# A second feed-forward layer whose first product goes by a 2x2x2 Strassen scheme over pairs of chunks and of token blocks, with its weights converted right behind the attention

## The chip, the cores and the metric

The kernel runs on one core of one Trainium2 chip. The metric is the device time of one execution in microseconds, as the median of several runs. The kernel's output is the transposed result of the last layer.

## What is computed

A linear attention with decay over 4 batches, 8 heads, 768 positions and 48 dimensions gives x (3072 tokens x 384). Two feed-forward layers follow, each with d_model 384 and d_ff 2048; they differ in the gate:

```python
state = zeros(B, H, D, D)
for t in range(S):
    cur = (u * k[t]) outer v[t]
    y[t] = r[t] @ (state + cur)
    state = w[t] * state + k[t] outer v[t]
x = y as (B*S, H*D)
h = x @ w_in1;  x = (h * clip(h + 3, 0, 6) / 6) @ w_out1
h = x @ w_in2;  out = (h * sigmoid(h)) @ w_out2
```

All inputs are float32. The feed-forward products use the fp32r form of TensorE. To keep the accuracy, every operand is held as two parts: a high part (the value rounded by a copy into fp32r) and a low part (the value less the high part). A product of two such operands is three matmuls: high by high, high by low, low by high.

## The kernel before

**Tiles.** The tokens are cut into six blocks j of 512 (four batches of 128 positions); the attention works through 24 groups of 128 tokens. Each layer cuts d_ff into 16 chunks fc of 128 and d_model into three k-chunks of 128. All feed-forward matmuls but those of the start are 128x128 by 128x512. For one block and one chunk, `mm1` (L842, matmuls at L858) makes the hidden tile h in a PSUM bank with 3 k-chunks x 3 = 9 matmuls; the gate and `split` (L886) make the high part gh and the low part gl; `mm2` (L865, matmuls at L880) adds them into three accumulators of 128 output columns with 9 more. PSUM has eight banks here: two of tag "h" for the hidden tiles, three "att" and three "acc" for attention and accumulators.

**Stages.** Attention groups (`attention`, L604) are interleaved with the first layer's blocks (`block1`, L900). The first layer's result goes to a DRAM scratch `x2d` and comes back with `load_x2` (L927), which makes its high and low parts. `block2` (L941) is the second layer: 6 blocks x 16 chunks x 18 matmuls, its gate one pass of ACT (L950) and then a cast (L891) and a subtraction (L893) on DVE.

**Weights.** A chunk of both weights of a layer arrives as pairs of 32-bit words; `load_w` (L466) turns them into float32 with three DVE passes over 768 columns (L32, L38, L44) and `split_w` (L499) into high and low parts with an ACT copy (L504) and a DVE subtraction (L505). The first `LATE_W = 4` chunks (L510) of the second layer go to a pool of their own, the rest into slots that the first layer's weights leave. All of them wait for `last_att` (L995): in the kernel before, all work planned up to the fifth block of the first layer.

**Checks.** `check_decay` (L792, two ACT passes at L800) and `check_weights` (L808) look for inputs out of the supported range while the second layer runs; a one-column matmul at the end makes a flag of them.

**Order.** Nothing is issued in the order of the source. Every piece of work is an `op` with a cost in ns for each engine that may do it and a key (its due place), and `Plan.order` (L263) fixes the order of each engine beforehand. It simulates the engines with these costs and, for an engine that comes free, takes among the operations that could start first the one with the smallest key:

```python
first = min(t for t, _ in able)
t, op = min((x for x in able if x[0] <= first), key=lambda x: (x[1].key, x[1].n))
```

A buffer slot is free when its last user has ended by that count. So a changed cost or key moves instructions on every engine. In `block2` the key of chunk fc of block j is 16 * (6 + j) + fc, and its second product stands `MM2 = 1.5` later, so that on PE the second product of one chunk follows the first product of the next.

Of the kernel before, what the change touches and what calls it, by code (L numbers as in the profile page):

```python
# [344 lines left out]
def tile_decay_attention_mlp2(  # L345
# [26 lines left out]
    C = 128  # L372
# [93 lines left out]
    def load_w(layer, fc, key, where="wp", after=(), whole=False):  # L466
# [28 lines left out]
        wts[layer, fc] = (val,)  # L495
        if not whole:
            split_w(layer, fc, key, where)

    def split_w(layer, fc, key, where="wp"):  # L499
# [290 lines left out]


    def check_decay(g, key, after):  # L792
        ws = Part(new("late", "cw", 2, [PD, SEQ + 1], f"cw{g}"))
        op({"SP": 470}, key - 2, lambda e: e.dma_start(out=ws.ap, in_=wseq_in[g]),
           writes=[ws], data=2000.0, after=after)
        off = Part(new("late", "off", 1, [PD, NP, C], f"off{g}"))

        def reach(e):
            for i, sign in enumerate((1.0, -1.0)):
                e.activation(  # L800
                    off.ap, ws.ap[:, 0:SEQ].rearrange("p (a b) -> p a b", b=SEG)[:, :, 1:],
                    AF.Relu, scale=sign, bias=-W_REACH - sign,
                    accum_out=stray.ap[:PD, 2 * g + i:2 * g + i + 1],
                )

        op({"ACT": 1560}, key, reach, [ws], [off, stray])
# [117 lines left out]
                out=x2d[j].ap[:, c, :], in_=x2.ap  # L924
            ), [x2], [x2d[j]], data=730.0)

    def load_x2(j, key, after):  # L927
        raw = Part(new("late", "xr", 2, [128, KC, N], f"xr{j}"))
        op({"SP": 470}, key, lambda e: e.dma_start(out=raw.ap, in_=x2d[j].ap),
           [x2d[j]], [raw], data=2200.0, after=after)  # L930
        new_x(1, j)
        xh, xl = x_parts[1, j]
        op({"DVE": 960, "ACT": 1450}, key + 1, lambda e: (
            e.activation(xh.ap, raw.ap, AF.Copy) if e is nc.scalar
            else e.tensor_copy(xh.ap, raw.ap)
        ), [raw], [xh])
        op({"DVE": 1755, "POOL": 4200}, key + 1, lambda e: e.tensor_tensor(
            xl.ap, raw.ap, xh.ap.bitcast(F32), op=ALU.subtract
        ), [raw, xh], [xl])

    def block2(j, key):  # L941
        acc = [
            Part(new("ps", "acc" if j % 2 else "att", 3, [128, N], f"acd{j}_{c}"))
            for c in range(KC)
        ]
        for fc in range(FC):
            kk = key + fc
            h = mm1(1, j, fc, kk)
            g = Part(new("gp", "g", 2, [128, N], f"g2_{j}_{fc}"))
            op({"ACT": 595}, kk, lambda e, g=g, h=h: e.activation(g.ap, h.ap, AF.Silu), [h], [g])  # L950
            gh, gl = split(g, f"2_{j}_{fc}", kk, {"DVE": 430}, {"DVE": 690})
            turn = {FC - 3: (-0.5, 0.05, 0.1), FC - 2: (0.2, 0.3, 1.4), FC - 1: (1.2, 1.3, 1.5)}
            mm2(1, fc, gh, gl, acc, kk + MM2, [
                key + FC - 1 + x for x in turn.get(fc, ())
            ] if j == NCH - 1 else ())
        for c in range(KC):
            o = Part(new("late", "o", 3, [128, N], f"o{j}_{c}"))
            op({"ACT": 595, "DVE": 690}, key + FC, lambda e, c=c, o=o: (
                e.activation(o.ap, acc[c].ap, AF.Copy) if e is nc.scalar
                else e.tensor_copy(o.ap, acc[c].ap)  # L960
            ), [acc[c]], [o])
            op({"SP": 470}, key + FC, lambda e, c=c, o=o: e.dma_start(
                out=out_t[c * 128:(c + 1) * 128, :].rearrange("p (b s) -> p b s", b=B)[
                    :, :, j * C:(j + 1) * C
                ],
                in_=o.ap.rearrange("p (b s) -> p b s", b=B),
            ), [o], data=730.0)


    MM2 = 1.5  # L970
    WHOLE = (0,)
    WHOLE_FC = 8
    loads = {g: load_group(g, FIRST + g) for g in range(B)}
    begun = [o for o in plan.ops if "SP" in o.engs]
    begun[0].data += 450.0
# [4 lines left out]
    for j in range(NCH):  # L980
        new_x(0, j)
        for i in range(B):
            key = -100.0 + i if j == 0 else FC * (j - 1) + (j == 1) * 3.0 + i * 3.3
            attention(j * B + i, key)
        if j == 0:
            for fc in range(FC):
                if fc == WHOLE_FC:
# [11 lines left out]
    for fc in range(LATE_W, FC):  # L999
        load_w(1, fc, FC * (NCH - 1) + 2 + 2 * fc)  # L1000
    for j in range(NCH):
        load_x2(j, FC * (NCH + j) - 6.0, last_att)
        block2(j, FC * (NCH + j))
    begin = FC * (NCH + 1)
    for i in range(NG):
        check_decay(i, begin + 2.5 * i, last_att)
    if WW == 2:
        for i in range(2 * FC):
            check_weights(i // FC, i % FC, begin + 1 + 2 * i, last_att)


    total = Part(flags.tile([128, 1], F32, name="total"))
    ones = Part(flags.tile([128, 1], F32, name="ones"))
    bad = Part(flags.tile([1, 1], I32, name="bad"))
    late = FC * (2 * NCH - 1) + 3.0
    op({"DVE": 100}, late, lambda e: e.memset(ones.ap, 1.0), [], [ones], after=last_att)
    op({"DVE": 230}, late, lambda e: e.tensor_reduce(total.ap, stray.ap, axis=AX.X, op=ALU.add),
       [stray], [total])
    op({"DVE": 150}, late, lambda e: e.tensor_scalar(total.ap, total.ap, 0.0, None, op0=ALU.is_le),
       [total], [total])  # L1020
    pf = Part(new("ps", "att", 3, [1, 1], "pf"))
    op({"PE": 60}, late, lambda e: e.matmul(pf.ap, total.ap, ones.ap, start=True, stop=True),
       [total, ones], [pf])
    op({"DVE": 150}, late, lambda e: e.tensor_scalar(bad.ap, pf.ap, 128.0, None, op0=ALU.is_lt),
       [pf], [bad])
# [101 lines left out]
```

## Time and profile before

| | before |
|---|---|
| median of 3 runs | 913.15 us (912.92 to 913.53) |
| the profiled execution | 913.38 us |
| its span (first to last instruction) | 911.7 us |
| PE busy | 902.6 us, 99% of the span |
| DVE busy | 570.7 us, 63% |
| ACT busy | 331.6 us, 36% |
| POOL busy | 62.1 us, 7% |
| TensorE clock granted | 0.998 |

The profile comes from one execution. Busy times are sums over an engine's instructions; matmuls are pipelined, so that the time of one matmul in a list of groups is longer than its step in a row of them. PEld is the weight load of TensorE, which overlaps the matmuls. A wait shows as idle time before an instruction, with the instruction that ended it.

### The profile page before, as it was taken

To read this page: it belongs to the slowest core of one execution; us is meant where nothing else is said; L and a number is where in the kernel's file an instruction comes from. 1 tells how busy PE (TensorE), PEld (TensorE's weight loads), DVE (VectorE), ACT (ScalarE), POOL (GpSimd) and SP (SyncE) were. 2 spreads that over 40 slices of the span, in tenths; PEclk is the share of its full clock that TensorE was granted. 3 is DMA by queue.
4 is the path that set the end of the run, shared out by engine and by line. 5 is a ranking of instruction groups with operands and counts; after the bars stand their busy time and mean duration, and the time that the engine had idled before them with its cause. 6 is when DMAs were issued, how large, how long until landed. Compare 5 with 4: busy or idle time off the path is not lost.

```text
span 911.7 us, 13804 instructions
## 1 busy us (share of the span) xinstructions
PE 902.6 (99%) x5570; PEld 721.7 (79%) x5570; DVE 570.7 (63%) x926; ACT 331.6 (36%) x785; POOL 62.1 (7%) x52
## 2 busy tenths in 40 slices
PE   9999999999999999999999999999999999999997
PEld 7546778888888878888888888888888888888886
DVE  8999999867676766664478878544544543222221
ACT  6645474314332332331145756323233321212111
POOL 1514003100020110000000000000000000000000
PEclk9999999999999999999999999999999999999999
DMA  9945324313221311110076765644644500100001
GB/s 304 362 119 167 127 75 128 108 44 94 89 87 43 109 42 41 65 33 1 24 242 190 217 202 173 202 150 162 208 140 169 176 35 1 35 1 6 30 1 36
DMA packets 39604, 101.11 MB, mean 111 GB/s; under 512 B 3697, under 2 KB 16113, under 8 KB 39537
## 3 DMA queue, kind: packets, MB, share of 16 engines
q1 hardware_dynamic: 39536, 100.20, 34.1%
q8 instruction: 44, 0.72, 0.3%
q14 instruction: 24, 0.19, 0.1%
HBM read 90.75 MB, written 9.44 MB: 110 GB/s over the span
## 4 chain that ended last, share of the span: by engine, by line
PE 91%; DVE 7%; issue 1%; ACT 0%; POOL 0%; DVEq 0%; POOLq 0%; ACTq 0%
PE h L858 41%; PE acd L880 22%; PE acc L880 19%; PE py L720 3%; PE pa L641 2%; PE filler L588 1%; DVE val L38 1%; PE pkv L753 1%; PE acc L871 1%; PE pk L654 1%; DVE val L44 1%; DVE g L913 1%; DVE spare L707 0%; DVE pre L616 0%; DVE val L32 0%
## 5 line engine op out<-in xcount | busy, mean ns | idle before, releaser
L858 PE MATMUL h<-x,w 128*128 128x512 f32 x1584 | 390.4, 391 | 0.0
L858 PEld LDWEIGHTS h<-x,w 128*128 128x128 f32 x1584 | 295.8, 188 | 62.4 <-issue 0.4
L891 DVE CAST gh<-g 128x512 fp32r<-128x512 f32 x161 | 70.5, 438 | 196.0 <-ACT g L950 191.7
L880 PE MATMUL acd<-gh,w 128*128 128x512 f32 x576 | 192.7, 389 | 0.0
L880 PE MATMUL acc<-gh,w 128*128 128x512 f32 x528 | 180.2, 393 | 0.0
L950 ACT ACTIVATE g<-h 128x512 f32<-128x512 f32 x96 | 57.5, 599 | 260.1 <-PE h L858 235.9
L893 DVE TENSOR_TENSOR gl<-g,gh 128x512 fp32r<-128x512 f32 x184 | 128.6, 701 | 4.8 <-ACT gh L890 0.3
L880 PEld LDWEIGHTS acd<-gh,w 128*128 128x128 f32 x576 | 108.1, 188 | 22.5
L911 ACT ACTIVATE g<-h 128x512 f32<-128x512 f32 x96 | 57.2, 596 | 180.3 <-PE h L858 171.6
L880 PEld LDWEIGHTS acc<-gh,w 128*128 128x128 f32 x528 | 99.1, 188 | 22.0 <-issue 0.6
L913 DVE SCALAR_TENSOR_TENSOR g<-g,h 128x512 f32<-128x512 f32 x96 | 65.4, 682 | 80.3 <-ACT g L911 80.1
L880 PE MATMUL acd<-gl,w 128*128 128x512 f32 x288 | 112.0, 389 | 0.0
L880 PE MATMUL acc<-gl,w 128*128 128x512 f32 x264 | 103.1, 390 | 0.0
L880 PEld LDWEIGHTS acd<-gl,w 128*128 128x128 f32 x288 | 54.0, 188 | 11.2
L880 PEld LDWEIGHTS acc<-gl,w 128*128 128x128 f32 x264 | 49.6, 188 | 10.3 <-DVE gl L893 0.6
L675 POOL TENSOR_TENSOR ruk<-rkn,u_bc 128x384 f32<-128x384 f32 x20 | 34.0, 1702 | 284.9 <-DVE bb L690 165.5
L704 ACT ACTIVATE a<-ident,bb 128x128 f32<-128x128 f32 x160 | 49.8, 391 | 0.0
L707 DVE COPY_PREDICATED a<-causal,pa 128x512 f32<-128x512 int32 x42 | 29.4, 734 | 5.8 <-PE pa L641 4.9
L816 DVE TENSOR_SCALAR_CACHE_REDUCE cval<-cval 128x768 f32<-128x768 f32 x32 | 30.3, 947 | 2.3 <-ACT cval L28 2.3
L800 ACT ACTIVATE off<-cw 112x512 f32<-112x512 f32 x48 | 30.2, 630 | 0.8
L28 ACT ACTIVATE cval<-craw 128x768 f32<-128x768 f32 x32 | 28.9, 903 | 1.5 <-DVE cval L816 1.5
L616 DVE TENSOR_TENSOR_SCAN pre<-ws,ind 112x516 f32<-112x516 f32 x21 | 27.4, 1303 | 1.6 <-DMA ws<-in_wseq_dram 1.6
(108 smaller groups left out, 723.3 us busy)
## 6 DMA issues: line engine op xcount, KB each, us to landing
raw<-in_moe_w_dram SPq DMA_DIRECT2D x32, 768.0 KB, 5.4
craw<-in_moe_w_dram SPq DMA_DIRECT2D x32, 768.0 KB, 4.4
rk<-in_rk_dram SPq DMA_DIRECT2D x21, 448.0 KB, 3.7
rkn<-in_rkn_dram SPq DMA_DIRECT2D x20, 384.0 KB, 3.2
cw<-in_wseq_dram SPq DMA_DIRECT2D x24, 226.2 KB, 2.8
ws<-in_wseq_dram SPq DMA_DIRECT2D x22, 226.2 KB, 2.8
vn<-in_vn_dram SPq DMA_DIRECT2D x22, 224.0 KB, 2.7
x2d<-x SPq DMA_DIRECT2D x18, 256.0 KB, 2.4
```

The lines of the kernel that those rows point to most:

```text
L675: op({"POOL": 1000}, key, lambda e: e.tensor_tensor(ruk.ap, of(rkn, 0, H), u_bc.ap, op=ALU.mult), [rkn, u_bc], [ruk], port=True)
L704: e.activation(a.ap[:, p, :], ident.ap, AF.Copy, scale=bs.ap[:, 2 * p + i])
L707: op({"DVE": 610}, key, lambda e, a=a, pa=pa[i]: e.copy_predicated(a.ap, causal.ap.bitcast(I32).unsqueeze(1).to_broadcast([128, NP, C]), pa.ap
L800: e.activation(off.ap, ws.ap[:, 0:SEQ].rearrange("p (a b) -> p a b", b=SEG)[:, :, 1:], AF.Relu, scale=sign, bias=-W_REACH - sign, accum_ou ...
L816: op({"DVE": 600}, key, lambda e: e.tensor_scalar(val.ap, val.ap, TINY, 0.0, op0=ALU.is_lt, op1=ALU.add, accum_out=stray.ap[:, col:col + 1 ...
L858: e.matmul(h.ap, a.ap[:, 0, kc * 128:(kc + 1) * 128], b.ap[:, kc, :], start=(kc == 0 and i == 0), stop=(kc == KC - 1 and i == 2),)
L880: e.matmul(acc[c].ap, a.ap[:, 1, sl], b.ap, start=(fc == 0 and i == 0), stop=(fc == FC - 1 and i == 2),)
L891: else e.tensor_copy(gh.ap, src.ap)
L893: op(lo_engs, key, lambda e: e.tensor_tensor(gl.ap, src.ap, gh.ap.bitcast(F32), op=ALU.subtract), [src, gh], [gl], port=True)
L911: op({"ACT": 595}, kk, lambda e, g=g, h=h: e.activation(g.ap, h.ap, AF.Relu, bias=3.0), [h], [g])
L913: op({"DVE": 690}, kk, lambda e, g=g, h=h: e.scalar_tensor_tensor(g.ap, g.ap, 6.0, h.ap, op0=ALU.min, op1=ALU.mult), [g, h], [g])
L950: op({"ACT": 595}, kk, lambda e, g=g, h=h: e.activation(g.ap, h.ap, AF.Silu), [h], [g])
```

## The change

Two chunks 2q and 2q+1 and two token blocks 2p and 2p+1 make a **quad** (p, q); there are 3 **pairs** of blocks with 8 quads each. `pair2` (L1052 of the changed kernel) takes the place of `block2`. For the first two of the three k-chunks it takes the 2 x 2 x 2 product (chunks x k-chunks x blocks) in Winograd's form of Strassen's scheme: seven products in place of eight, of sums of weight tiles by sums of token tiles. The third k-chunk stays four plain products. A quad's hidden tiles so take 11 products of three matmuls, 33 in place of 36; the second product stays 36.

- All eleven products go into the two banks of tag "h", as x (two products), y1 (two), y2, y3 (two), y4 (two), y5 (two). An ACT copy takes x after its first product (r1) and after its second (u2). Six DVE adds take the others, from PSUM with r1, u2 or t5, into four tiles g; the gate and the two splits follow.
- `load_pair` converts two chunks at once and makes three sums of weight tiles for each pair of chunks (four DVE operations of 128 columns, L545 to L548), which `split_s` splits.
- `load_x2` loads two blocks, makes the token sums t1 to t4 and splits nine terms of 128x512; they are held once and rewritten from pair to pair.
- `LATE_W` is 3, `last_att` holds the attention alone, so that the second layer's weights are loaded and converted right behind the last attention groups; the decay checks and the weight checks have other keys (18 weight checks in the second pair, 14 in the third) and the decay checks other buffers, and the flag's matmul uses an "h" bank.

```diff
         if WW == 2:
-            op({"DVE": 480}, key, lambda e: upper_bits(e, raw.ap, val.ap.bitcast(I32)),
+            op({"DVE": 555 if layer else 480}, key, lambda e: upper_bits(e, raw.ap, val.ap.bitcast(I32)),
...
-                op({"DVE": 870}, key, lambda e, step=step: step(e, raw.ap, val.ap.bitcast(I32)),
+                op({"DVE": 955 if layer else 870}, key, lambda e, step=step: step(e, raw.ap, val.ap.bitcast(I32)),
...
-    LATE_W = 4
+    LATE_W = 3
+
+    def split_s(q, s, key, where):
...
+        op({"ACT": 450}, key, lambda e: e.activation(hi.ap, s.ap, AF.Copy), [s], [hi])
+        op({"DVE": 550}, key, lambda e: e.tensor_tensor(
+            lo.ap, s.ap, hi.ap.bitcast(F32), op=ALU.subtract
+        ), [s, hi], [lo], port=True)
...
+    def load_pair(q, key, where="wp", after=()):
+        a, b = 2 * q, 2 * q + 1
+        load_w(1, a, key, where, after=after, whole=None)
...
+        split_w(1, a, key, where)
+        load_w(1, b, key + 1, where, after=after, whole=None)
...
+            e.tensor_tensor(s3, s3, a21, op=ALU.subtract)
+            e.tensor_tensor(a21, a21, a22, op=ALU.add)
+            e.tensor_tensor(s2, a22, s3, op=ALU.subtract)
+            e.tensor_tensor(s4, s4, s2, op=ALU.subtract)
...
+        split_w(1, b, key + 1, where)
+        split_s(q, s, key + 1, where)
...
-    def block2(j, key):
...
+    def product(h, w, x, key, start, stop):
...
+            for i, (a, b) in enumerate(((wh, xh), (wh, xl), (wl, xh))):
+                e.matmul(
+                    h.ap, of(a.ap), b.ap, start=start and i == 0, stop=stop and i == 2,
...
+    def pair2(p, key):
...
+            product(x, a_(a, 0), terms["b11"], k + KEYS[0], True, True)
+            copy(x, r1, k + KEYS[0])
+            product(x, s_(q, 0), terms["t2"], k + KEYS[1], False, True)
+            copy(x, u2, k + KEYS[1])
+            product(y1, a_(a, 1), terms["b21"], k + KEYS[2], True, False)
+            product(y1, a_(a, 2), terms["b31"], k + KEYS[2], False, True)
+            add(y1, r1, g[0, 0], k + KEYS[2])
+            product(y2, a_(b, 0), terms["t1"], k + KEYS[3], True, True)
+            add(y2, u2, t5, k + KEYS[3])
+            product(y3, s_(q, 1), terms["t3"], k + KEYS[4], True, True)
+            add(y3, u2, u2, k + KEYS[4])
+            product(y3, a_(b, 2), terms["b32"], k + KEYS[4], False, True)
+            add(y3, t5, g[1, 1], k + KEYS[4])
+            product(y4, s_(q, 2), terms["b22"], k + KEYS[5], True, False)
+            product(y4, a_(a, 2), terms["b32"], k + KEYS[5], False, True)
+            add(y4, t5, g[0, 1], k + KEYS[5])
+            product(y5, a_(b, 1), terms["t4"], k + KEYS[6], True, False)
+            product(y5, a_(b, 2), terms["b31"], k + KEYS[6], False, True)
+            add(y5, u2, g[1, 0], k + KEYS[6])
...
+    QUAD_KEYS = (0.0, 0.3, 0.6, 0.9, 1.2, 1.8, 2.4, 3.5)
...
-    last_att = [o for o in plan.ops if o.key < 1e6]
-    for fc in range(LATE_W):
-        load_w(1, fc, FC * (NCH - 1) + 3 * fc, "lw", after=last_att)
+    load_pair(0, FC * (NCH - 1), "lw", last_att)
     block1(NCH - 1, FC * (NCH - 1))
...
+    load_x2(0, FC * NCH, last_att)
+    for q in range(1, FC // 2):
+        load_pair(q, FC * (NCH - 1) + 2 + 4 * q)
+    begin = FC * (NCH + 1) - 3
```

On PE in the steady state of the second layer, block 3 before: the last matmuls of chunk 5's first product, and the second product of chunk 4 behind it (h1_3_5 is the hidden tile of layer 1, block 3, chunk 5, counted from 0; x0 and x1 are the high and low parts of the tokens, acd3_0 an accumulator).

```order
L858 MATMUL h1_3_5_6842<-x0_1_3_6192,w1_5_5081 128x512 x2
L858 MATMUL h1_3_5_6842<-x1_1_3_6214,w1_5_5081 128x512
L858 MATMUL h1_3_5_6842<-x0_1_3_6192,w1_5_5081 128x512
L880 MATMUL acd3_0_6736<-gh2_3_4_6840,w1_4_5026 128x512
L880 MATMUL acd3_0_6736<-gl2_3_4_6846,w1_4_5026 128x512
```

The same engine with the change, quad (2, 3): x's first product, then what stands ahead of x's second one in the same bank h0 (xt0 to xt2 hold the token terms, a last 0 or 1 for the high and low part; s2 holds the sums of weight tiles).

```order
L1045 MATMUL h0_2_3_7713<-xt01_4665,w1_6_5142 128x512
L1045 MATMUL h0_2_3_7713<-xt00_4640,w1_6_5142 128x512
L1128 MATMUL acd5_0_7504<-gh2_2_2_11_7675,w1_5_5069 128x512
L1128 MATMUL acd5_0_7504<-gl2_2_2_11_7680,w1_5_5069 128x512
L1128 MATMUL acd5_0_7504<-gh2_2_2_11_7675,w1_5_5069 128x512
L1128 MATMUL acd5_1_7514<-gh2_2_2_11_7675,w1_5_5069 128x512
L1128 MATMUL acd5_1_7514<-gl2_2_2_11_7680,w1_5_5069 128x512
L1128 MATMUL acd5_1_7514<-gh2_2_2_11_7675,w1_5_5069 128x512
L1045 MATMUL h0_2_3_7713<-xt10_5232,s2_5076 128x512
L1045 MATMUL h0_2_3_7713<-xt11_5241,s2_5076 128x512
```

First and second products before went in pieces of nine; now they change places every three or six matmuls, and a bank "h" is read and written again after six matmuls that go elsewhere.

On PE at the first quad of the second layer with the change: both of x's products in bank h0, then y1 in h1.

```order
L1045 MATMUL h0_0_0_5247<-xt01_4665,w1_0_4543 128x512
L1045 MATMUL h0_0_0_5247<-xt00_4640,w1_0_4543 128x512
L1045 MATMUL h0_0_0_5247<-xt10_5232,s0_4620 128x512
L1045 MATMUL h0_0_0_5247<-xt11_5241,s0_4620 128x512
L1045 MATMUL h0_0_0_5247<-xt10_5232,s0_4620 128x512
L1045 MATMUL h1_0_0_5262<-xt00_4640,w1_0_4543 128x512
```

Here no matmul of another bank stands between x's first product and its second, between which ACT copies the bank.

On DVE while the second layer starts, before (block 0): the casts and subtractions of the hidden tiles gh and gl, and between them the conversion of chunk 10's weights (bits and w).

```order
L891 CAST gh2_0_5_5365<-g2_0_5_5360 128x512
L32 TENSOR_SCALAR bits1_10_5370<-raw1_10_5279 128x768
L893 TENSOR_TENSOR gl2_0_5_5372<-g2_0_5_5360,gh2_0_5_5365 128x512
L38 SCALAR_TENSOR_TENSOR bits1_10_5370<-raw1_10_5279,bits1_10_5370 128x768
L44 SCALAR_TENSOR_TENSOR bits1_10_5370<-raw1_10_5279,bits1_10_5370 128x768
L891 CAST gh2_0_6_5403<-g2_0_6_5394 128x512
L893 TENSOR_TENSOR gl2_0_6_5408<-g2_0_6_5394,gh2_0_6_5403 128x512
L505 TENSOR_TENSOR w1_10_5401<-bits1_10_5370,w1_10_5401 128x768
```

The same engine with the change, quad (0, 3); L1077 is an add from an "h" bank, sw6 and s6 the sums of weight tiles.

```order
L1077 TENSOR_TENSOR g2_0_3_00_5719<-h1_0_3_5689,r1_0_3_5682 128x512
L545 TENSOR_TENSOR sw6_5667<-sw6_5667,bits1_13_5695 128x128
L546 TENSOR_TENSOR bits1_13_5695<-bits1_13_5695 128x128
L547 TENSOR_TENSOR sw6_5667<-bits1_13_5695,sw6_5667 128x128
L548 TENSOR_TENSOR sw6_5667<-sw6_5667 128x128
L1077 TENSOR_TENSOR t5_0_3_5735<-h2_0_3_5711,u2_0_3_5704 128x512
L937 TENSOR_TENSOR gl2_0_3_00_5744<-g2_0_3_00_5719,gh2_0_3_00_5737 128x512
L1077 TENSOR_TENSOR u2_0_3_5704<-h3_0_3_5731,u2_0_3_5704 128x512
L505 TENSOR_TENSOR w1_13_5742<-bits1_13_5695,w1_13_5742 128x768
L523 TENSOR_TENSOR s6_5749<-sw6_5667,s6_5749 128x384
L32 TENSOR_SCALAR bits1_14_5767<-raw1_14_5669 128x768
L1077 TENSOR_TENSOR g2_0_3_11_5772<-h3_0_3_5731,t5_0_3_5735 128x512
```

Before, DVE read only what ACT had taken out of PSUM; now four adds that empty a bank stand among the passes of the weight conversion. The conversion was at chunk 10 in the sixth chunk of block 0, and is at chunks 13 and 14 in the fourth quad (chunks 6 and 7) of the first pair.

## Rows read from the trace of the kernel before

**Rows 1.** The page: busy time of each engine; the granted clock in 40 slices.

```profile
PE 902.6 (99%) x5570; PEld 721.7 (79%) x5570; DVE 570.7 (63%) x926; ACT 331.6 (36%) x785; POOL 62.1 (7%) x52
...
PEclk9999999999999999999999999999999999999999
```

**Rows 2.** The page: the chain that ended last, by engine.

```profile
PE 91%; DVE 7%; issue 1%; ACT 0%; POOL 0%; DVEq 0%; POOLq 0%; ACTq 0%
```

**Rows 3.** Busy time by stretches of the span, columns in the first line.

```profile
core 0: us, PE busy (x) PEld busy (x) DVE busy (x) ACT busy (x) POOL busy (x), PEclk, DMA share, GB/s
0.00:50.00 50.00, 47.56 (x482) 32.10 (x486) 46.27 (x67) 31.53 (x122) 15.10 (x16) 1.00 0.99 330
100.00:150.00 50.00, 49.63 (x438) 38.88 (x437) 48.59 (x77) 29.95 (x65) 4.91 (x4) 1.00 0.31 97
512.00:577.00 65.00, 65.00 (x288) 53.60 (x287) 49.86 (x72) 39.74 (x91) 0.00 (x0) 1.00 0.62 202
643.00:708.00 65.00, 65.00 (x289) 53.81 (x288) 32.02 (x60) 20.88 (x31) 0.00 (x0) 1.00 0.50 170
```

**Rows 4.** The chain in order of time: start us, us, what.

```profile
520.00 4.08 PE acd L880 x18
524.08 2.04 PE h L858 x9
526.12 2.04 PE acd L880 x9
```

**Rows 5.** Groups by line and shape: busy us, mean ns of one, idle before.

```profile
L893 DVE TENSOR_TENSOR gl<-g,gh 128x512 fp32r<-128x512 f32 x184 | 128.6, 701 | 4.8 <-ACT gh L890 0.3
...
L891 DVE CAST gh<-g 128x512 fp32r<-128x512 f32 x161 | 70.5, 438 | 196.0 <-ACT g L950 191.7
L913 DVE SCALAR_TENSOR_TENSOR g<-g,h 128x512 f32<-128x512 f32 x96 | 65.4, 682 | 80.3 <-ACT g L911 80.1
L950 ACT ACTIVATE g<-h 128x512 f32<-128x512 f32 x96 | 57.5, 599 | 260.1 <-PE h L858 235.9 <-issue 24.1
...
L800 ACT ACTIVATE off<-cw 112x512 f32<-112x512 f32 x48 | 30.2, 630 | 0.8
...
L38 DVE SCALAR_TENSOR_TENSOR bits<-raw,bits 128x768 int32<-128x768 int32 x24 | 22.9, 954 | 0.3
...
L505 DVE TENSOR_TENSOR w<-bits,w 128x768 fp32r<-128x768 f32 x24 | 22.9, 952 | 5.9 <-ACT w L504 5.8
...
L32 DVE TENSOR_SCALAR bits<-raw 128x768 int32<-128x768 int32 x24 | 13.5, 562 | 0.1
...
L771 DVE TENSOR_TENSOR s<-pkv,s 48x192 f32<-48x192 f32 x32 | 11.3, 352 | 6.1 <-PE pkv L753 5.9
L742 DVE TENSOR_TENSOR x<-py,x 128x384 fp32r<-128x384 f32 x20 | 11.1, 556 | 2.9 <-ACT x L738 2.6
```

**Rows 6.** The timeline: start us, us, engine line op, [idle before <-releaser].

```profile
67.81 1.49 DVE L631 TENSOR_TENSOR kh<-rk,suf 112x512 f32<-112x512 f32 x1
...
69.35 0.75 PEld L641 LDWEIGHTS pa<-rh,kh 48*128 48x128 f32 x12 [1.38 <-DVE kh L631]
69.35 0.83 PE L641 MATMUL pa<-rh,kh 48*128 48x128 f32 x10 [0.55 <-DVE kh L631]
...
883.09 2.00 PEld L858 LDWEIGHTS h<-x,w 128*128 128x128 f32 x9
883.31 2.20 PE L858 MATMUL h<-x,w 128*128 128x512 f32 x9
...
885.60 0.60 ACT L950 ACTIVATE g<-h 128x512 f32<-128x512 f32 x1 [3.48 <-PE h L858]
```

**Rows 7.** DMA issues: KB each, median us from issue to landing.

```profile
raw<-in_moe_w_dram SPq DMA_DIRECT2D x32, 768.0 KB, 5.4
```

**Rows 8.** The timeline at the end, columns as in rows 6.

```profile
905.53 0.39 PE L880 MATMUL acd<-gh,w 128*128 128x512 f32 x1
905.95 0.60 ACT L959 ACTIVATE o<-acd 128x512 f32<-128x512 f32 x1 [0.76 <-PE acd L880]
```

More of the change, by code (lines that the diff above doesn't have):

```diff
@@ L495, in load_w @@
         wts[layer, fc] = (val,)
-        if not whole:
+        if whole is False:
             split_w(layer, fc, key, where)
@@ L792, in check_decay @@
     def check_decay(g, key, after):
-        ws = Part(new("late", "cw", 2, [PD, SEQ + 1], f"cw{g}"))
+        ws = Part(new("late", "o", 3, [128, SEQ + 1], f"cw{g}"), lambda t: t[:PD])
         op({"SP": 470}, key - 2, lambda e: e.dma_start(out=ws.ap, in_=wseq_in[g]),
            writes=[ws], data=2000.0, after=after)
-        off = Part(new("late", "off", 1, [PD, NP, C], f"off{g}"))
+        off = Part(new("late", "o", 3, [128, SEQ + 1], f"off{g}"), lambda t: (
+            t[:PD, 0:N].rearrange("p (a b) -> p a b", b=C)
+        ))
         def reach(e):
@@ L925, in block1 @@
             ), [x2], [x2d[j]], data=730.0)
[L927 to L939, printed above, removed]
@@ L941, in block2 @@
-    def block2(j, key):
-        acc = [
-            Part(new("ps", "acc" if j % 2 else "att", 3, [128, N], f"acd{j}_{c}"))
-            for c in range(KC)
-        ]
[L946 to L967, printed above, removed]
@@ new lines, in tile_decay_attention_mlp2, with finish @@
+    total = Part(flags.tile([128, 1], F32, name="total"))
+    ones = Part(flags.tile([128, 1], F32, name="ones"))
+    bad = Part(flags.tile([1, 1], I32, name="bad"))
+    def finish(late):
+        op({"DVE": 100}, late, lambda e: e.memset(ones.ap, 1.0), [], [ones], after=last_att)
+        op({"DVE": 230}, late, lambda e: e.tensor_reduce(total.ap, stray.ap, axis=AX.X, op=ALU.add),
+           [stray], [total])
+        op({"DVE": 150}, late, lambda e: e.tensor_scalar(total.ap, total.ap, 0.0, None, op0=ALU.is_le),
+           [total], [total])
+        pf = Part(new("ps", "h", 2, [1, 1], "pf"))
+        op({"PE": 60}, late, lambda e: e.matmul(pf.ap, total.ap, ones.ap, start=True, stop=True),
+           [total, ones], [pf])
+        op({"DVE": 150}, late, lambda e: e.tensor_scalar(bad.ap, pf.ap, 128.0, None, op0=ALU.is_lt),
+           [pf], [bad])
@@ L970, in tile_decay_attention_mlp2 @@
+    ORDER = ((0, 0), (1, 1), (0, 1), (1, 0))
+    LAST_ORDER = ((0, 0), (1, 0), (1, 1), (0, 1))
+    QUAD_KEYS = (0.0, 0.3, 0.6, 0.9, 1.2, 1.8, 2.4, 3.5)
+    LAST_KEYS = (0.0, 0.3, 0.6, 0.9, 1.2, 1.8, 1.5, 3.5)
+    LAST_TURN = {2: (0.0, 0.1, 1.2), 3: (0.0, 0.1, 0.3)}
     MM2 = 1.5
@@ L972, in tile_decay_attention_mlp2 @@
     WHOLE_FC = 8
+    last_att = []
     loads = {g: load_group(g, FIRST + g) for g in range(B)}
@@ L983, in tile_decay_attention_mlp2 @@
             key = -100.0 + i if j == 0 else FC * (j - 1) + (j == 1) * 3.0 + i * 3.3
+            n = len(plan.ops)
             attention(j * B + i, key)
+            last_att += plan.ops[n:]
         if j == 0:
@@ L994, in tile_decay_attention_mlp2 @@
                     split_w(0, fc, FC * (max(WHOLE) + 1) + fc - 3.0)
-    last_att = [o for o in plan.ops if o.key < 1e6]
-    for fc in range(LATE_W):
-        load_w(1, fc, FC * (NCH - 1) + 3 * fc, "lw", after=last_att)
+    load_pair(0, FC * (NCH - 1), "lw", last_att)
     block1(NCH - 1, FC * (NCH - 1))
[L999 to L1004, printed above, removed]
+    new_terms()
+    load_x2(0, FC * NCH, last_att)
+    for q in range(1, FC // 2):
+        load_pair(q, FC * (NCH - 1) + 2 + 4 * q)
+    begin = FC * (NCH + 1) - 3
     for i in range(NG):
         check_decay(i, begin + 2.5 * i, last_att)
[L1007 to L1025, printed above, removed]
+    weights = list(range(2 * FC if WW == 2 else 0))
+    for p in range(NCH // 2):
+        if p:
+            load_x2(p, FC * (NCH + 2 * p), last_att)
+        for _ in range((0, 18, 14)[p]):
+            if weights:
+                i = weights.pop(0)
+                check_weights(i // FC, i % FC, begin + FC + 2 * i, last_att)
+        pair2(p, FC * (NCH + 2 * p))
     with tc.manual_schedule():
```

143 lines of the change are left out of this document (added).

## The prediction, made before the changed kernel was run

> **What bounds the kernel now.** I read the page's busy shares first. TensorE is busy 902.6 of 911.7 us, at full granted clock in every slice, and no other engine passes 63% [rows 1]. A busy PE need not be a bounding PE, so the chain of work that ended last comes next: 91% of it is PE, 7% DVE [rows 2]. By stage, PE has small gaps up to 150 us and none at all after 440 us: 65.00 of 65 us in the stretch where the second layer begins [rows 3]. There DVE is busy 49.86 of 65 us, later about half. Last, the chain in order of time gives the price of a matmul: nine of them take 2.04 us, in the first product and in the second alike, and 18 take 4.08 [rows 4]. That is 0.2267 us each, which I call a slot. (The durations of single matmul rows, near 0.39 us, overlap and aren't used.) So the second layer is 6 x 16 x 18 = 1,728 slots = 391.7 us with no wait inside it. A slot removed there is worth 0.2267 us, until something else makes PE wait.
>
> **What is removed.** A quad (two chunks, two token blocks) had 4 x 18 = 72 matmuls and has 33 + 36 = 69. With 8 x 3 = 24 quads that is 72 slots: 72 x 0.2267 = **-16.3 us**. Nothing before the last steps of the first layer's fifth block moves on PE, so this is the whole gain.
>
> **What is added beside PE.** Per quad DVE gets six adds that read a product in PSUM. The nearest row is the fused multiply of the same size with one operand in PSUM, 0.682 us, and a 384-column add from PSUM takes 0.556 [rows 5]; I take 0.69. ACT gets two copies, at the 0.60 of a pass out of PSUM [rows 5]. In the second and third pair of blocks DVE then has 6 x 0.69 + 4 x 0.70 + 2 or 3 casts x 0.44, about 8 us, and 10 with the weight checks, in a quad of 69 x 0.2267 = 15.6 us. ACT has 2 x 0.60 + 4 x 0.60 and some casts, some 5 us, 6.5 with checks. Both hide under PE as sums. What doesn't follow from sums is whether each result comes in time, because all eleven products share two PSUM banks.
>
> **The price of a bank turn.** In the last matmuls of h, the ninth began at 883.31 + 8 x 0.2267 = 885.12 and ACT took its bank at 885.60: 0.48 us later [rows 6]. The pass takes 0.60, or 0.69 on DVE. PE's next weight load began 0.05 after the result it waited for (the DVE row ends at 69.30, the load starts at 69.35), and the matmul 0.22 after its load [rows 6]. So a matmul into the same bank can begin 1.35 us (ACT) or 1.44 us (DVE) after the last one began. One slot of that is its own; every matmul into another place hides one more. With none between, PE loses 1.12 or 1.21 us; with three, 0.44; with six (1.36 us), nothing, with 0.15 to 0.24 us to spare.
>
> Counted in the order: the usual quad has six matmuls in each tight place (the first product to the second in x's bank, y1 to y3, y3 to its continuation). The first quad has none between x's two products: 1.12 us, and then a decay check of 2 x 0.63 us [rows 5] stands on ACT ahead of the second copy and ends some 0.2 after that copy could begin: **+1.3**. The second quad of each later pair has three between x's second product and y2: 2 x 0.44 = **+0.9**.
>
> **Weights converted under the first pair.** Each chunk still costs DVE 0.56 + 2 x 0.954 + 0.952 us [rows 5], and each pair of chunks now four small subtractions of 128 columns and one of 384. The small ones have no row; 192 columns take 0.352 [rows 5], the line through that and the 0.701 of 512 columns gives 0.28, and I keep 0.23 (in proportion to the columns) to 0.35 as bounds. From the end of the first layer to the fifth quad's last add the order holds 32 adds, 19 low parts, 7 casts, 31 conversion passes and 20 of these small ones: 72 us of DVE work, where PE has 306 slots = 69.4 us. DVE has run at 97% (48.59 of 50) beside a PE at 99% [rows 3]. At 97% it would need 74.3 us, 4.9 more than PE. Some 2.9 us of that is free, since the last add of a quad has 18 to 27 matmuls before its bank is wanted. Bounds 0 and 4.9; I take **+1.0**, because the order puts 9 to 12 extra matmuls in front of just those adds that stand behind conversions.
>
> **What moves at no cost.** The nine token terms of a new pair add 10 us to DVE in one quad (17.0 against 15.6), between quads with 8 to 10; the terms are rewritten as each old one is read for the last time. Weight loads land 5.4 us after issue [rows 7] and are converted two to three quads (30 us) before use; the decay loads that now stand between them on SP's queue can't use that up. The flag's one-column product takes a bank that is free for 18 matmuls. The end is as before: the last accumulator's copy starts 0.42 us after the last matmul begins [rows 8], and two of the three outputs are out before it.
>
> **Sum.** 16.3 - 1.3 - 0.9 - 1.0 = 13.1 us. The profiled execution took 913.38 us (span 911.7), so 900.3; the median of the runs lies 0.23 under it, at 913.15: **900.0 us**.
>
> **Rivals.**
> - Everything hides (the 3.2 us of waits are not there). For it: the order was made with waits in mind and PE waits for nothing in 440 to 906 us now. Against: the first quad's two products stand back to back in one bank. 913.15 - 16.3 = 896.8.
> - DVE bounds the first pair and both changes of pair. For it: 72 us of work in 69.4. Against: the quads after it hold 8 us each, so the lag heals. Then 1.3 + 0.9 + 4.9 + 2 x 1.5 (17.0 against 15.6) = 10.1 us come back: 907.0.
> - **Slower: two banks don't carry it.** If one further DVE pass of 0.70 us stands ahead of the add in each tight turn, a turn is 2.14 us against the 1.59 of seven slots, 0.55 lost in three turns of 24 quads: 40 us, and 937. It decides at 16.3 / 72 = 0.23 us per turn. For it: there's one of these passes or a longer one in the queue at most times in the first pair. Against: in the later pairs the order shows only the add itself, or the add before it, between the product and the turn. The Trainium skill (Perfetto Trace Analysis, Matmuls) asks that independent matmul groups rotate through different PSUM banks so that emptying one overlaps the next group; here x's two products go on in one bank with a copy between. Read strictly, every quad would pay the bare turn of 1.12 us: 24 x 1.12 = 26.9, and 913.15 - 16.3 + 26.9 = 923.8, slower too. By rows 6 the six matmuls between cover it.
> - The clock falls. PE idled 2.4 of the first 50 us, with single waits of over half a microsecond, and the granted clock stayed at 1.00 [rows 3, 6], the 2.4 GHz level. At 1.2 GHz a quad would take 15.6 us longer by my estimate of twice a slot, so one or two quads would eat the gain. The Trainium skill (TensorE: Matmul & The Clock Gate, A second HAM failure mode) tells of a kernel that cycled through PSUM banks and whose clock went back and forth for its small idle times. No wait that I expect is longer than those in rows 3.
>
> **Chances.** My forecast, waits of 1.8 to 5.5 us in all (898.6 to 902.4): 0.62. All hidden: 0.13. DVE bounds, 902.4 to 910: 0.18. Within 0.2% of before (1.8 us, about what a measurement can tell): 0.02. Slower, by bank turns 0.04 and by the clock 0.01. The range, 896.6 to 905.0, takes the first two whole and half of the third, 0.84 together; it covers both bounds of the DVE term. Faster 0.93, same 0.02, slower 0.05.
>
> **What would show it.** Right: PE rows of the second layer still at 2.04 us for nine; 69 slots from one quad's first product to the next's; PE waits only at the first quad (over 1 us, for ACT's copy), in the second quad of the later pairs (0.4 us), and in the first pair for DVE; DVE over 95% there and near 60% after; clock 1.00. Wrong: waits of PE for DVE or ACT in nearly every quad of the later pairs (then the turn is dearer than 1.44 us), an add well over 0.69 us, a gap of some 1.5 us at each change of pair, or a lower clock in any stretch.

## The result and the profile after

The changed kernel takes **901.94 us** (median, 901.69 to 902.88) against 913.03 us for the kernel before: ratio 0.9881, 95% interval 0.9864 to 0.9898. It is 1.2% faster. The forecast was 900.0 us, 896.6 to 905.0; the time lies inside, 1.9 us above the point. That it came this near is in part luck: as the parts below show, errors of both signs met.

The page after, busy times, clock and chain by engine, against [rows 1, 2]:

```profile
span 900.1 us, 14055 instructions
...
PE 889.8 (99%) x5498; PEld 708.2 (79%) x5498; DVE 668.5 (74%) x1109; ACT 398.5 (44%) x904; POOL 61.7 (7%) x52
...
PEclk9999999999999999999999999999999999999999
...
PE 90%; DVE 8%; issue 1%; DMA 1%; ACT 0%; POOL 0%; DVEq 0%; POOLq 0%; ACTq 0%
```

PE has exactly 72 matmuls fewer (5,570 to 5,498). DVE has 97.8 us more work and ACT 66.9, and PE is still the chain. Who PE waited for from 505 us to the end (engine, line, waited for: us in total, times, longest):

```profile
PE h L1045 <- ACT r L1074: 0.7, 1, 0.7
```

The timeline has it (start us, us, engine line op, [idle before <-releaser]):

```profile
511.20 0.84 PE L1045 MATMUL h<-xt,w 128*128 128x512 f32 x3
...
512.08 0.60 ACT L1074 ACTIVATE r<-h 128x512 f32<-128x512 f32 x1 [1.60 <-PE h L1045]
...
512.73 0.96 PE L1045 MATMUL h<-xt,s 128*128 128x512 f32 x3 [0.69 <-ACT r L1074]
```

The third matmul of x's first product starts at 511.20 + 2 x 0.2267 = 511.66, the fourth at 512.73: 0.85 us more than a slot. This is the one wait in the whole second layer, and yet the change gave 11.5 us in the profiled executions (913.38 to 901.88) where 16.3 us of slots were removed. The chain in order of time shows where else time went. A steady quad of the second pair (start us, us, what), against [rows 4]:

```profile
683.99 2.04 PE h L1045 x9
...
686.71 1.36 PE h L1045 x6
688.07 1.36 PE acd L1128 x6
689.43 0.70 PE h L1045 x3
690.14 0.69 PE acd L1128 x3
690.83 2.81 PE h L1045 x12
693.64 4.11 PE acd L1128 x18
```

Six matmuls take 1.36 us, as priced, but three take 0.70 where 3 x 0.2267 is 0.68, and twelve take 2.81 in place of 2.72. **No wait is shown; the matmuls themselves follow each other more slowly**, at 231 to 240 ns. It is so in every quad, in the same places: from y3's second product over y4 to y5's first, the products that read the third pair of token-term tiles (b22, t4, b32), and up to eight matmuls beyond. Waits aside, 495 steps of the second layer are 229 ns or longer. A quad takes 15.79 us, not 69 x 0.2267 = 15.64. From the first matmul of the layer to the last, 382.05 us pass.

The stretch of the first pair, busy us by engine (columns as in [rows 3]), and the groups of the new work (busy us, mean ns, idle before):

```profile
512.80:582.20 69.40, 69.40 (x303) 56.93 (x304) 61.83 (x105) 44.08 (x89) 0.00 (x0) 1.00 0.38 123
```

```profile
L1077 DVE TENSOR_TENSOR g<-h,t 128x512 f32<-128x512 f32 x48 | 32.7, 688 | 16.1 <-PE h L1045 15.7
...
L546 DVE TENSOR_TENSOR bits<-bits 128x128 f32<-128x128 f32 x8 | 2.3, 292 | 0.3
...
L1074 ACT ACTIVATE r<-h 128x512 f32<-128x512 f32 x24 | 14.4, 598 | 51.0 <-PE h L1045 50.9
```

DVE had 7.6 us to spare there and PE was busy all 69.40 us. The prices of the passes were right: 0.69 us for an add, 0.29 for a small one, 0.60 for a copy.

The end, to be read against [rows 8] (timeline):

```profile
893.26 0.39 PE L1128 MATMUL acd<-gh,w 128*128 128x512 f32 x1
894.35 1.25 ACT L1141 ACTIVATE o<-acd 128x512 f32<-128x512 f32 x2 [1.90 <-DMA out_dram<-o]
```

ACT's copy starts 1.09 us after the last matmul began, where it was 0.42, it waited for an output's DMA, and two copies stand there, not one. From the last matmul to the end of the span 6.82 us pass, 0.68 more than before (911.67 - 905.53 = 6.14).

### The profile page after: what moved, and what is told of

Its sections match the earlier page's. It is cut to its first block, busy times and chain, and to the rows that moved or that the text cites. A ratio compares the mean times of both kernels' runs of the same rounds, so it can differ in the third digit from the quotient of the medians.

```text
span 900.1 us, 14055 instructions
## 1 busy us (share of the span) xinstructions
PE 889.8 (99%) x5498; PEld 708.2 (79%) x5498; DVE 668.5 (74%) x1109; ACT 398.5 (44%) x904; POOL 61.7 (7%) x52
## 4 chain that ended last, share of the span: by engine, by line
PE 90%; DVE 8%; issue 1%; DMA 1%; ACT 0%; POOL 0%; DVEq 0%; POOLq 0%; ACTq 0%
PE acd L1128 21%; PE h L1045 20%; PE h L902 20%; PE acc L924 20%; PE py L762 3%; PE pa L683 2%; PE filler L630 1%; DVE val L38 1%; PE pkv L795 1%; PE acc L915 1%; PE pk L696 1%; DVE val L44 1%; DVE g L957 1%; DMA out_dram<-o 1%; DVE val L32 0%
## 5 line engine op out<-in xcount | busy, mean ns | idle before, releaser
L902 PE MATMUL h<-x,w 128*128 128x512 f32 x720 | 178.8, 392 | 0.0
L902 PEld LDWEIGHTS h<-x,w 128*128 128x128 f32 x720 | 133.7, 188 | 28.5 <-issue 0.4
L1045 PE MATMUL h<-xt,w 128*128 128x512 f32 x576 | 152.3, 393 | 0.0
L1045 PEld LDWEIGHTS h<-xt,w 128*128 128x128 f32 x576 | 108.2, 188 | 24.3
L955 ACT ACTIVATE g<-h 128x512 f32<-128x512 f32 x96 | 57.2, 596 | 151.6 <-PE h L902 142.6
L1120 ACT ACTIVATE g<-g 128x512 f32<-128x512 f32 x96 | 60.4, 630 | 117.0 <-DVE g L1077 116.7
L935 DVE CAST gh<-g 128x512 fp32r<-128x512 f32 x121 | 53.4, 441 | 49.0 <-PE acd L1128 27.8
L1128 PEld LDWEIGHTS acd<-gl,w 128*128 128x128 f32 x288 | 54.0, 188 | 11.5
L1045 PE MATMUL h<-xt,s 128*128 128x512 f32 x216 | 61.2, 392 | 0.7 <-ACT r L1074 0.7
L934 ACT ACTIVATE gh<-g 128x512 fp32r<-128x512 f32 x63 | 39.6, 631 | 19.9 <-DVE g L957 16.4
L1045 PEld LDWEIGHTS h<-xt,s 128*128 128x128 f32 x216 | 40.5, 188 | 9.8 <-ACT r L1074 1.1
```

Of the source, the lines that this page charges most:

```text
L902: e.matmul(h.ap, a.ap[:, 0, kc * 128:(kc + 1) * 128], b.ap[:, kc, :], start=(kc == 0 and i == 0), stop=(kc == KC - 1 and i == 2),)
L934: e.activation(gh.ap, src.ap, AF.Copy) if e is nc.scalar
L935: else e.tensor_copy(gh.ap, src.ap)
L1045: e.matmul(h.ap, of(a.ap), b.ap, start=start and i == 0, stop=stop and i == 2, skip_group_check=True,)
L1120: op({"ACT": 595}, kk - 2, lambda e, t=t: e.activation(t.ap, t.ap, AF.Silu), [t], [t])
L1128: e.matmul(accs[n][c].ap, l.ap[:, 1, sl], r.ap, start=first and z == 0, stop=final and z == 2,)
```

## The experiments

Each ran beside the kernel before on one chip, and its ratio is to that. The first four ask what makes matmuls slow without a wait.

**1. Thirty-two bytes.** The program's addresses gave the idea: the tiles of the weights, the first two pairs of token tiles, gh and gl all start at 544 modulo 2,048 (what is left of the byte address in the partition when 2,048 is taken off as often as it goes). Only the slow tiles, allocated behind others in the late pool, start elsewhere, at 128. The edit adds 32 bytes to one of those others, the buffer sw of 1,536 bytes, and so moves every tile of the pool behind it.

```diff
-        s = Part(new("late", "sw", 1, [128, 3, 128], f"sw{q}"))
+        s = Part(new("late", "sw", 1, [128, 3 * 128 + 8], f"sw{q}"), lambda t: (
+            t[:, 0:384].rearrange("p (a b) -> p a b", b=128)
+        ))
```

> One buffer ahead of the third pair of token-term tiles (b22, t4, b32) is 32 bytes larger, so these tiles start at 190,624 and 200,864 bytes of each partition instead of 190,592 and 200,832; every instruction and its order stay. In the changed kernel's trace the matmuls that read these tiles, and some five to eight behind them, follow each other at 231 to 240 ns where all others take 227: 0.14 us in every quad, 3.5 us in all. Theory (the place of the tile, by its start modulo 64 bytes, which is 0 there and 32 for every other matmul operand): the slow steps vanish, nine matmuls take 2.04 us everywhere, a quad 15.64 instead of 15.79 us, and the time falls by 3.5 us, to about 898.4 us or 0.9840 of the kernel before. Rival (the frequent change of PSUM banks, or the products themselves): the slow steps stay in the same places, 901.9 us. Second rival (the pool near the end of the partition): the same, 901.9 us.

900.76 us, ratio 0.9864 (0.9848 to 0.9881). Neither: the layer takes 380.97 us, 1.1 less, with 397 steps of 229 ns or longer left, in another pattern. The same quad, in the chain:

```profile
688.66 0.69 PE h L1047 x3
689.36 0.69 PE acd L1130 x3
690.05 2.77 PE h L1047 x12
```

Twelve take 2.77. Instructions and order being the same, the place of a tile behind the pad matters; its start modulo 64 alone isn't the rule, and this expectation failed.

**2. Two tiles change places.**

```diff
-                new("xp", f"x{m}", 2, [128, KC, N], f"xt{i}{m}", F32R) if i < 2
+                new("xp", f"x{m}", 2, [128, KC, N], f"xt{i}{m}", F32R) if i > 0
```

> The tiles of b11, b21, b31 change places with those of b22, t4, b32: the first now start at multiples of 64 bytes behind the other late tiles, the second lie where the first layer's tokens lay. Theory (place of the tile): the slow steps move with the place, to x's first product, to both of y1 and to the second of y5; y3's second product and y4 run at 227 ns; 12 of 33 first-product matmuls read the tiles, as before, so the time stays within 1 us of 901.9. Rival (bank changes or the products): the slow steps stay at y3's second product, y4 and y5.

903.6 us (one run). The chain of a steady quad:

```profile
684.18 1.37 PE acd L1128 x6
685.55 2.09 PE h L1045 x9
...
691.08 0.68 PE h L1045 x3
...
692.44 2.74 PE h L1045 x12
...
699.28 0.70 PE h L1045 x3
```

x's second product and y1 (nine matmuls) take 2.09 where the change had 2.04 (the row at 683.99 above), y3's second product is back at 0.68, and y4 and y5 fall to 2.74, of which the 0.02 too many are in y5's second product. That one reads a moved tile now, as does x's first product of the next quad, with 0.70. The other late tiles, which the pad had moved too, stayed where they were. **The slowness goes with the place of the tile that the matmul reads, not with the product or the bank.** The time is not within the 1 us expected, since the planner moved other things too: PE now waits four times around the first quad, 1.7 us.

**3. Everything shifted by 32 bytes.**

```diff
     stray_t = flags.tile([128, 2 * NG + 2 * FC], F32, name="stray")
+    flags.tile([128, 8], F32, name="gap")
```

> A gap of 32 bytes ahead of all other buffers shifts every matmul operand by 32 bytes: tokens, weights, gh and gl to multiples of 64, the third pair of token-term tiles away from them; their distance to the weights modulo 64 stays 32. If the start of the moving operand alone decides, all feed-forward matmuls but those of the third tiles become slow: at 5 to 9 ns for each of some 3,100 of them, 15 to 28 us, 917 to 930 us. If the difference to the other operands (the weights above all) decides, nothing changes: slow steps at the same products, 901.9 us. If it is a multiple of 128 bytes that hurts, nothing is slow: 898.4 us.

901.87 us, ratio 0.9877 (0.9861 to 0.9894). In the chain:

```profile
689.34 0.70 PE h L1046 x3
690.04 0.69 PE acd L1129 x3
690.73 2.81 PE h L1046 x12
```

0.70 and 2.81 again, in the same places; the others, now at multiples of 64, stay fast. In this run the slow tiles lie at 190,624 and 200,864, the very addresses of experiment 1, and are as slow as in the change (508 steps of 229 ns or longer, the layer 382.06 us), while there 1.1 us was won. So **it is not the address but how the tile lies to the other operands.**

**4. The tile where the others are, modulo 2,048.** The pad of experiment 1 with `3 * 128 + 104`.

> As the 32-byte pad, with 416 bytes: the third pair of token-term tiles now starts at 191,008 and 201,248 bytes, 544 modulo 2,048 like all other matmul operands (weights, the other tokens, gh, gl all start at 544 modulo 2,048; in the changed kernel these tiles start at 128, with the 32-byte pad at 160). So far: shifting everything but the difference left every slow step in place, changing places moved them with the tile, and 32 bytes changed their pattern and took 1.1 us. Theory (what counts is how the tile lies to the other operands of neighbouring matmuls, up to 2,048 bytes): all steps of the second layer are 227 ns, 3.5 us less than the change, about 898.4 us. Rival (the region, beyond 190,000 bytes of the partition): the slow steps stay, 900.7 to 902 us.

898.63 us, ratio 0.9846 (0.9832 to 0.9859), 0.2 us from what was expected. The same quad:

```profile
688.00 0.68 PE h L1047 x3
688.68 0.68 PE acd L1130 x3
689.36 2.72 PE h L1047 x12
692.08 4.08 PE acd L1130 x18
```

Every step of this quad is 0.2267 us, a quad 15.64 us, the layer 378.52 us: 3.53 less than in the change. In the whole layer 13 steps of some 1,660 are still 229 ns or longer. The tiles are still behind 191,000 bytes, so the region isn't the cause. Open: which operand they must agree with (the weights loaded meanwhile, or the tokens of the matmul ahead), and modulo how much. A weight operand is a slice of its tile, at a multiple of 512 bytes from the tile's start, so the operands themselves now agree modulo 512 and not modulo 2,048.

**5. Output tiles of their own at the end.**

```diff
+                if j == NCH - 1 and c < 2:
+                    o = Part(new("late", f"ts{c}", 1, [128, N], f"o{j}_{c}"))
+                else:
+                    o = Part(new("late", "o", 3, [128, SEQ + 1], f"o{j}_{c}"), lambda t: t[:, 0:N])
```

> Two of the last block's three output tiles use buffers of their own (those of two token sums, free by then) instead of the three that all outputs share. In the changed kernel ACT's copy of the last two accumulators started 1.09 us after the last matmul began, and waited for an output's DMA; in the kernel before 0.42 us. Theory (the output buffers set the tail): the copy starts 0.42 us after it, and one copy rather than two stands behind the last matmul: 0.65 us less, about 901.3 us. Rival (the end is set by the transfers themselves, all six on one queue): no difference above 0.2 us.

901.45 us, ratio 0.9876 (0.9859 to 0.9892). The interval can't tell this from the change; the timeline can:

```profile
893.22 0.39 PE L1128 MATMUL acd<-gh,w 128*128 128x512 f32 x1
893.69 0.60 ACT L1144 ACTIVATE o<-acd 128x512 f32<-128x512 f32 x1 [0.81 <-PEq L1214]
```

The copy starts 0.47 us behind the last matmul and is alone; the end follows at 6.1 us (899.3 - 893.22) in place of 6.82. The three shared tiles were the cause.

**6. The change without its early weights.**

```diff
+    last_att = [o for o in plan.ops if o.key < 1e6]
     load_pair(0, FC * (NCH - 1), "lw", last_att)
```

> The change without its second part: the second layer's weights may be converted only behind all that is planned up to the first layer's fifth block, as before; their first conversion comes some nine chunks later in the order (fc 4 of block 5 in place of fc 11 of block 4). In the changed kernel DVE was busy 61.83 of 69.40 us behind the first quad's start, and PE waited for it nowhere. Theory (DVE has these 7.6 us to spare, and the early conversion is not needed): within 0.5 us of 901.9. Rival (the early conversion is what keeps DVE from bounding the first pair): the work of some four chunks, about 4 x 3.5 us plus sums, falls into the first pair, and PE waits 4 to 9 us there: 906 to 911 us.

905.44 us, ratio 0.9921 (0.9905 to 0.9936): 3.5 us dearer by the medians, so the theory fell, and the rival has the sign right but not the place. The waits of PE from 505 us on:

```profile
PE h L1045 <- ACT r L1074: 2.2, 1, 2.2
PE acc L924 <- DVE gl L937: 0.6, 1, 0.6
```

Both are at the hand-over from the first layer to the first quad, where conversion passes and splits of token terms stand on DVE and ACT between the last gates and the first copies. They are 2.8 us against 0.7 in the change, and the profiled execution, the fastest of four, is 2.4 us dearer; what the medians have beyond that no trace shows. Behind 528 us the list has no wait of PE, with DVE between 14.1 and 14.7 of 16 us up to 592 us. The edit isn't about weights alone: the same list holds back the loads of the tokens and the checks (the first token load went out at 457.7 us, in the change at 393.0), so how much of the 3.5 us the weights have is open.

**7. The kernel before with early weights alone.** The lines of the change around `last_att`, in the kernel before.

> The kernel before with the second part of the change alone: the second layer's weights are converted right behind the attention, with the plain second layer. Theory (PE waits for nothing from 440 us on in the kernel before, and the conversion has room in either place): no change, within 0.3 us of 913. Rival (the conversion itself is worth time, or delays the first layer's fifth block on DVE): 1 us or more to either side.

912.77 us, ratio 0.9998 (0.9989 to 1.0008). Alone, the second part is worth nothing; with the scheme its list `last_att` saves 3.5 us by the medians of experiment 6.

**8. The price of a turn.**

```diff
-            op({"DVE": 690}, key, lambda e: e.tensor_tensor(
-                dst.ap, src.ap, other.ap, op=ALU.add
-            ), [src, other], [dst])
+            first = r1 if dst is other else dst
+            def run(e):
+                for t in (first, dst):
+                    e.tensor_tensor(t.ap, src.ap, other.ap, op=ALU.add)
+            op({"DVE": 690}, key, run, [src, other], [first, dst] if dst is other else [dst])
```

> Each of the six adds of a quad runs twice on DVE (the first pass into the same tile, or into r1 where the add is in place), 0.69 us more per bank emptied, with the order of every engine as it was. It tests the price of a bank turn on which the prediction rests. In a steady quad of the changed kernel y3's continuation starts 0.42 us after the add that empties its bank has ended, and y1's bank is free 0.6 us before y3 wants it. Theory (turns are as priced: 1.44 us and the length of what DVE does ahead, against seven steps of 0.227): y3's continuation comes 1.25 to 1.4 us late in every quad, 30 to 34 us, and the first pair, where DVE has 61.8 us of work in 69.4 and gets 18.6 more, some 6 us on top: about 938 us, 928 to 945. Rival (banks have more room than that and DVE's sum counts, 12 of 15.8 us in the later pairs): only the first pair grows, by some 11 us: 913 us.

938.68 us, ratio 1.0283 (1.0264 to 1.0302). PE waits in all quads:

```profile
PE h L1045 <- DVE u L1081: 10.5, 21, 1.3
PE h L1045 <- DVE g L1081: 5.5, 24, 0.4
```

A steady quad takes 16.9 us, 1.1 more: 0.49 are lost at y3's start and 0.62 at its continuation, where the theory had 1.25 to 1.4 us at the continuation alone. The first pair of blocks takes 16.0 us more than in the change, the later two 10.6 and 10.2. So the total fits the theory's 938, but not its split, 30 to 34 us in the quads and some 6 on top in the first pair. The list has 18 us of waits in all where 36.7 us are lost: it counts a wait from the modelled end of the matmul ahead, and the first step behind a wait is longer too (at the first quad of the change a listed 0.7 us cost 0.96). In the change, the timeline of quad (1, 3) has the add that empties y3's bank, the next DVE pass, and y3's continuation:

```profile
688.30 0.69 DVE L1077 TENSOR_TENSOR u<-h,u 128x512 f32<-128x512 f32 x1
688.90 0.68 DVE L937 TENSOR_TENSOR gl<-g,gh 128x512 fp32r<-128x512 f32 x1
...
689.27 0.86 PE L1045 MATMUL h<-xt,w 128*128 128x512 f32 x3
```

So the tightest turn there has 0.28 us between the add and the next matmul, not the 0.42 of the expectation; one pass of 0.69 us more on each turn makes the scheme 2.8% slower than the kernel before, with DVE at 81%. With all these waits the granted clock was 0.998 over the span, as without them.

**9 and 10. The first quad.** In the first of these, x's first product is due earlier there; in the second, in addition, t1 and t3 of the first pair are split behind the first layer's last gate (`+ (2.2 if p == 0 and nm in ("t1", "t3") else 0.0)` on their keys).

```diff
-            KEYS = LAST_KEYS if end else QUAD_KEYS
+            KEYS = LAST_KEYS if end else FIRST_KEYS if p == q == 0 else QUAD_KEYS
...
+    FIRST_KEYS = (-1.0, 0.3, 0.6, 0.9, 1.2, 1.8, 2.4, 3.5)
```

> The first quad's first product x gets a key 1.0 lower, so that on PE it stands ahead of the nine matmuls of the first layer's chunk 14 and not behind them; nothing else moves. In the changed kernel x's second product lost 0.85 us there, waiting for ACT's copy. Theory (that wait is the bare turn of the bank): with nine matmuls between, it is gone. But y1 then wants the other bank, which DVE empties only at 512.53 us (the first layer's last gate stands behind the lower parts of three token terms), so PE waits there instead, 0.6 to 0.7 us: some 0.2 us are won, 901.7 us. Rival (PE loses the bare turn only, DVE is not late): 0.85 us less, 901.1 us.

> As the run with x's first product earlier, and in addition the token terms t1 and t3 of the first pair have a key behind the first layer's last gate, so that DVE empties the second bank before it splits them. Theory (both waits at the first quad are gone): PE waits for nothing over 0.1 us between 505 us and the end, 0.85 us less than the change, 901.1 us. Rival (DVE's lag moves to y2 or y3, which read t1 and t3): a wait of PE for a token term's lower part, no gain.

901.47 and 901.51 us (two runs each, both 0.9876, 0.9858 to 0.9894). In the profile of the first no wait of PE of 0.1 us is left from 505 us on, and the span is 0.6 us shorter: DVE had emptied the second bank in time, so by the trace the theory there was too gloomy and its rival right; the time lies between the two. The second puts a wait in for the add that empties y2's bank (t is t5), and wins nothing more:

```profile
PE h L1046 <- DVE t L1078: 0.2, 1, 0.2
```

**11 and 12. Together.** Pad of 416 bytes and output tiles; then with the edits of experiment 10 as well.

> The 416-byte pad and the separate output tiles of the last block together. Theory (independent terms): 898.63 less the 0.5 us that the second gave alone, 898.1 us, with only the first quad's wait of 0.7 us on PE left. Rival (they overlap): 898.6 us.

> The pad, the output tiles and the two edits at the first quad. Theory: 0.85 us less than pad and output tiles, 897.3 us, which is within 0.5 us of the sum of slots alone (913.15 - 16.3 = 896.8). Rival (the first quad's wait only moves): 898.1 us.

**897.40 us**, ratio 0.9831 (0.9818 to 0.9845), and **897.04 us**, 0.9828 (0.9815 to 0.9842). Both beat both kernels; between the two the runs can't decide. The first is 0.7 us under its theory: the end took 6.10 us, where it took 6.99 with the pad alone, and the second layer began 0.5 us earlier, for which no edit accounts. The last is 0.2 us above the 896.8 of the rival in which everything hides. Pad, tiles and the single edit of experiment 9, together, weren't run.

## Why the prediction was right, and where it was wrong

| term of the sum | predicted, us | measured, us |
|---|---|---|
| 72 slots removed | -16.3 | -16.3 |
| first quad, x's second product | +1.3 | +0.96 |
| second quads of later pairs | +0.9 | 0 |
| DVE under weight conversion | +1.0 | 0 |
| the end | 0 | +0.7 |
| slow matmuls beside the misplaced tiles | none | +3.5 |
| sum | -13.1 | -11.1 |

The measured terms leave 0.4 us to the -11.5 of the profiled executions; 0.3 of it came before the second layer, which in the profile after was reached earlier by that much at the same matmul count.

- **Slots.** Right. With the tiles moved, 69 matmuls take 15.64 us and PE's time is the slots and the first quad's wait.
- **The bare turn.** Predicted 1.12 us, measured 0.85 and 0.11 on the next step. ACT began 0.42 us after the last matmul, not 0.48, and PE 0.05 after the copy, without the further 0.22 that I put between load and matmul; behind the wait in [rows 6], too, load and matmul both start at 69.35. The 0.2 for the decay check fell away: the check did stand ahead of the second copy, but nothing waited for it.
- **Second quads.** Wrong. I gave y2 the bank of x. The timeline of quad (1, 1) has x's second product, ACT's copy of it, and y2:

```profile
652.26 0.84 PE L1045 MATMUL h<-xt,s 128*128 128x512 f32 x3
653.14 0.60 ACT L1074 ACTIVATE u<-h 128x512 f32<-128x512 f32 x1 [1.44 <-PE h L1045]
653.62 0.84 PE L1045 MATMUL h<-xt,w 128*128 128x512 f32 x3
```

  y2 starts at 653.62, while ACT reads x's bank until 653.74: it is in the other one. Buffers here are taken by whoever is ready, so a bank's next user must be read with its waits, not from turn-taking.
- **DVE in the first pair.** The step that compared 72 us of work with 69.4 of slots failed: it added up the lengths of rows. This is the stretch of those 306 slots, up to the end of the fifth quad's last add (columns as in [rows 3]):

```profile
517.44:587.08 69.64, 69.64 (x306) 57.04 (x304) 62.63 (x107) 41.44 (x82) 0.00 (x0) 1.00 0.37 119
```

  The lengths of these 107 rows of DVE add up to 69.7 us, near the 72; yet DVE was busy for 62.63, 90% and not over 95%. Rows that follow each other without a pause mostly overlap by 0.08 us: the add at 688.30 (experiment 8) is 0.69 long, and the next pass starts 0.60 behind it. For PE the prediction left row lengths out for this reason, for DVE it did not. Where there is too little room, PE waits at the hand-over, as in experiment 6.
- **The end.** "The end is as before" was wrong by 0.7 us: a pair of blocks now ends with six outputs through three tiles.
- **The missing term.** A slot was taken as 0.2267 us wherever it stands; beside the misplaced tiles it is up to 0.240. It was listed neither among the costs nor among what would show the prediction wrong, which names waits, dear adds and the clock; but two of the signs of being right, 2.04 us for nine and 69 slots a quad, were not met for it. This term alone is larger than all the waits that were listed, 3.2 us. That the time lies in the forecast's 898.6 to 902.4 is luck, then: of those 3.2 us only 0.96 came, and 4.2 came from two terms that the sum didn't have.
- **Rivals.** "Everything hides" missed by 5 us, and is nearly reached with three small edits. "Two banks don't carry it" was wrong for this kernel (PE waits once). Experiment 8 adds one pass to each turn and lands at 938.68, by the rival's 937, but not by its price: that was 0.55 us in three turns, 1.65 a quad, and a steady quad lost 1.1 in two turns, and a quad of the first pair 2.0 on average. It shows that such a pass makes the scheme slower; that the totals agree is chance. The rule of the Trainium skill (Perfetto Trace Analysis, Matmuls) on rotating banks, read strictly, gave 923.8; by the runs, six matmuls elsewhere are enough between two users of a bank. The clock stayed at 1.00, also in experiment 8.

## What to carry to other kernels

Price a turn of a bank as the last matmul's start to the reader's, the reader's pass and PE's restart (0.42 + 0.69 + 0.05 us here) and count the matmuls that go elsewhere meanwhile; that carries a scheme with two banks, but one more pass on each turn loses it. When PE is busy without a wait and still behind the count of its slots, compare the length of equal runs of matmuls in the chain, and look which tile the long ones read. Count DVE's work by busy time and not by adding up row lengths. After adding tiles behind odd-sized ones, check where they start.

## What the runs showed of the hardware

Matmuls of 128x128 by 128x512 in fp32r ran at 227 ns a step when the tiles of all operands started at the same place modulo 2,048 bytes (the weight operands being slices of theirs, at multiples of 512 bytes), and mostly at 231 to 240 ns when the moving operand's tile started 416 bytes short of it (128 against 544), without any wait in the trace; 32 bytes nearer, 397 in place of 495 steps were 229 ns or longer. Up to eight matmuls behind, which read other tiles, are long too. The Trainium skill (SBUF — State Buffer, Specifications (TRN2)) tells of lines of 16 bytes, with a penalty for each access that crosses into a new one. All tiles here start at multiples of 32 bytes, so that by this alone none should differ from another; the runs show a dependence on the distance between operands that the rule doesn't give.

DVE passes that stood back to back overlapped in their rows: 0.69 us long, 0.60 apart.
